# A cached-attention kernel on one core: two chunks of projection weights as two loads, two more chunks projected for all rows up front, and a warm-up that reads a constant

## The chip, the core and the metric

One NeuronCore of a Trainium2 chip. Time is device microseconds of one execution. The profile's "span" runs from the first to the last instruction of the core; most executions of these kernels take 1.7 to 1.9 us more than their span, and this difference ("time minus span") matters below. The engines are named as in the profile: PE (matrix engine; PEld are its weight loads), DVE, ACT, POOL, and SP, which issues nearly all DMA.

## The reference, cut to what matters

```python
# x (8, 32, 1024), k_cache and v_cache (8, 4, 8192, 128), wq (1024, 4096), wo (4096, 1024), all bf16
W = 2048                                                # the last 2048 positions of the cache
q = (x @ wq).reshape(B, Sq, 32, 128).transpose(0, 2, 1, 3)
k = repeat(k_cache[:, :, Sk - W:, :], 8); v = repeat(v_cache[:, :, Sk - W:, :], 8)
p = softmax(einsum("bhqd,bhkd->bhqk", q, k) * 128 ** -0.5)
out = einsum("bhqk,bhkd->bhqd", p, v).transpose(0, 2, 1, 3).reshape(8, 32, 4096) @ wo
```

## The kernel before

It works on 32 units (batch, key head). A unit is 16 key blocks: scores (`s_ps`), exponential on ACT, product with V (`o_ps`). Between them stand pieces of other work, such as the transposes of the next unit's keys (`tp`). "K2" is the key tile of unit 2, "V2" its value tile. Units 0 to 4 get their keys transposed by PE from `k_raw`.

The start matters here. The first group's weights come in eight chunks of 128 rows. Chunks 0 to 3 are projected for all 256 rows of x, chunks 4 to 7 only for the 128 rows that hold what the first unit needs (`Q_CUT = 4`); the rest is made up between the first score blocks (`q_rest`).

```python
Q_CUT = 4
N_WARM = (7, 0, 0)
V_HALVES = 29            # units from this one on load V as two halves
W_AT = (3, 3, 4, 4, ...) # after which unit's loads a later weight load is issued
...
    def load_v(self, ui, eng):
        ...
        n = self.KT // (2 if ui >= V_HALVES else 1)
        for j in range(0, self.KT, n):
            eng.dma_start(...)
...
    def start(self):
        warm = self.ps_s.tile([P, 512], FP32, name="warm_ps", tag="s_ps")
        wz = self.c1.tile([P, 512], BF16, name="wz")
        nc.vector.memset(wz[:, :], 0.0)
        ...
        nc.sync.dma_start(out=x_sb[:, 0, :], in_=xf[0:P, :])
        nc.scalar.dma_start(out=x_sb[:, 1, :], in_=xf[P:2 * P, :])
        wq0 = self.load_wq(0, 0, (1, 1, 2)) + self.load_wq(0, 1, (2, 1, 1))   # chunks per load
        for p in wq0[:4]:
            p()
        self.load_k(0, 0)          # first half of K0
        wq0[4]()
        wq0[5]()
        self.load_k(0, 1)
        self.load_v(0, nc.sync)
        self.load_k(1)
        self.load_v(1, nc.sync)
        ...
        def warm_up(n):
            for i in range(n):
                nc.tensor.matmul(warm[:, :], lhsT=wz[:, 0:P], rhs=wz[:, :], start=True, stop=True)
        warm_up(N_WARM[0])
        ... # x_turn: sixteen transposes of x, copied to xT
        for c in range(self.DC):                      # 8 chunks
            for h in range(self.rep):                 # 8 heads
                q_mm(c, h, 0, P if c >= Q_CUT else self.NQ)
            ...
            if c == self.DC - 3:
                ...
                k_turn(0)                             # transposes of K0, first half
                k_copy(0)
        k_turn(1)
        ...
        def q_rest(k):
            for h in (2 * k, 2 * k + 1):
                for c in range(Q_CUT, self.DC):
                    q_mm(c, h, P, self.NQ)
            q_copy("v", k, 1, self.B)
```

Of the kernel before, what the change touches and what calls it, by code (L numbers as in the profile page):

```python
# [11 lines left out]
BF16 = mybir.dt.bfloat16  # L12
# [3 lines left out]

RL_LIMIT = 1.0e22
RL_MIN = 1.0e-10
Q_CUT = 4
N_WARM = (7, 0, 0)  # L20
VA_ROW = 160
V_HALVES = 29

PE_T = (0, 1, 2, 3, 4)

# [79 lines left out]
class Fast:  # L105
# [93 lines left out]
    def load_v(self, ui, eng):  # L199
        b, g = self.units[ui]  # L200
        self.v_sb[ui] = self.vp.tile([self.P, self.KT, self.Dh], BF16, name="v_sb", tag="v")
        n = self.KT // (2 if ui >= V_HALVES else 1)
        for j in range(0, self.KT, n):
# [108 lines left out]
    def start(self):  # L312
        nc, P = self.nc, self.P
        warm = self.ps_s.tile([P, 512], FP32, name="warm_ps", tag="s_ps")
        wz = self.c1.tile([P, 512], BF16, name="wz")
        nc.vector.memset(wz[:, :], 0.0)
        x_sb = self.vp.tile([P, self.NT, self.D], BF16, name="x_sb", tag="v")
        xf = self.x.rearrange("b s d -> (b s) d")
        H = self.DC // 2

        nc.sync.dma_start(out=x_sb[:, 0, :], in_=xf[0:P, :])  # L321
        nc.scalar.dma_start(out=x_sb[:, 1, :], in_=xf[P:2 * P, :])
        wq0 = self.load_wq(0, 0, (1, 1, 2)) + self.load_wq(0, 1, (2, 1, 1))
        for p in wq0[:4]:
            p()
        self.load_k(0, 0)
        wq0[4]()
        wq0[5]()
        self.load_k(0, 1)
        self.load_v(0, nc.sync)  # L330
        self.load_k(1)
        self.load_v(1, nc.sync)
        self.weights = []
        for g in range(self.Hkv):
            if g + 1 < self.Hkv:
                self.weights += self.load_wq(g + 1, 0) + self.load_wq(g + 1, 1)
            if g:
                self.weights += self.load_wo(2 * g - 2) + self.load_wo(2 * g - 1)
        self.weights += self.load_wo(2 * self.Hkv - 2) + self.load_wo(2 * self.Hkv - 1)
        for ui in range(2, 4):  # L340
            self.load_unit(ui)
        for v in self.va:
            nc.gpsimd.memset(v[:, :, self.Dh:self.VW], 1.0)
        nc.gpsimd.memset(self.ones_c[:, :], 1.0)
        def warm_up(n):
            for i in range(n):
                nc.tensor.matmul(warm[:, :], lhsT=wz[:, 0:P], rhs=wz[:, :], start=True, stop=True)
        warm_up(N_WARM[0])


        def x_turn(half, pl, tag):
            ps = pl.tile([P, H, self.NT, P], BF16, name="xT_ps", tag=tag)
            for c in range(H):
                for t in range(self.NT):
                    c0 = (half * H + c) * P
                    nc.tensor.transpose(ps[:, c, t, :], x_sb[:, t, c0:c0 + P], self.ident[:, :])
            for i, copy in ((0, nc.vector.tensor_copy), (1, nc.scalar.copy)):
                c0 = half * H + i * H // 2
                copy(out=self.xT[:, c0:c0 + H // 2, :], in_=ps[:, i * H // 2:(i + 1) * H // 2, :, :].rearrange("p c t s -> p c (t s)"))

        x_turn(0, self.ps_m, "m")
        x_turn(1, self.ps_s, "s_ps")
        qs = [pl.tile([P, 2, self.NQ], FP32, name="q0_ps", tag=tag)
              for pl, tag in ((self.ps_o, "o_ps"), (self.ps_o, "o_ps"), (self.ps_m, "m"), (self.ps_m, "m"))]
        KT = self.KT
        tp = None

        def k_turn(half):
            for j in range(half * KT // 2, (half + 1) * KT // 2):
                nc.tensor.transpose(tp[:, j, :], self.k_raw[0][:, j, :], self.ident[:, :])  # L370

        def k_copy(half):
            sl = slice(half * KT // 2, (half + 1) * KT // 2)
            nc.vector.tensor_copy(out=self.kT[0][:, sl, :], in_=tp[:, sl, :])  # L374

        def q_mm(c, h, n0, n1):
            nc.tensor.matmul(qs[h // 2][:, h % 2, n0:n1], lhsT=self.wq_t[0, c // H][:, c % H, h * P:(h + 1) * P],  # L377
                             rhs=self.xT[:, c, n0:n1], start=(c == 0 and h % 2 == 0), stop=(c == self.DC - 1),
                             skip_group_check=True)

        for c in range(self.DC):
            for h in range(self.rep):
                q_mm(c, h, 0, P if c >= Q_CUT else self.NQ)
            if c == 0:
                warm_up(N_WARM[2])
                warm_sb = self.c1.tile([P, 8], BF16, name="warm_sb")
                nc.vector.tensor_copy(out=warm_sb[:, :], in_=warm[:, 0:8])
            if c == self.DC - 3:
                tp = self.ps_s.tile([P, KT, P], BF16, name="kf_ps", tag="s_ps")
                k_turn(0)  # L390
                k_copy(0)
        k_turn(1)

        def q_copy(eng, k, b0, b1):
            src = qs[k][:, :, :].rearrange("p h (b s) -> p b h s", b=self.B)[:, b0:b1, :, :]
            dst = self.q_view(0)[:, b0:b1, k * 2:(k + 1) * 2, :]
            (nc.vector.tensor_copy if eng == "v" else nc.scalar.copy)(out=dst, in_=src)  # L397
        for k, eng in ((0, "a"), (1, "v"), (2, "a"), (3, "v")):
            q_copy(eng, k, 0, 1)
        k_copy(1)  # L400
        self.va_copy(0)
# [6 lines that stand above are left out]
        self.q_rest = [lambda k=k: q_rest(k) for k in (0, 2, 3, 1)]  # L408
# [249 lines left out]
```

## Time and profile before

| | before |
|---|---|
| time, median of 6 executions | 186.74 us (186.40 to 186.98) |
| span of the profiled execution | 184.6 us |
| PE busy | 179.9 us, 97% |
| first scores | 13.38 us |

Lines of the page of before (the span; each engine with its busy us, share of the span and instructions; the engines of the chain that ended last):

```profile
span 184.6 us, 5089 instructions
...
PE 179.9 (97%) x2072; PEld 153.7 (83%) x2072; DVE 115.2 (62%) x267; ACT 131.8 (71%) x133; POOL 94.7 (51%) x150
...
PE 93%; DMA 4%; SPq 1%; DVE 1%; issue 0%
```

The last line is the chain of work that ended last: it is PE for 93% of the span, so a microsecond of PE saved anywhere without a new wait is a microsecond of the kernel. The 4% of DMA are the load of weights at the start that the chain runs through (2.12 to 8.65 us); PE itself stood still for the last 0.87 us of it. PE's timeline of before shows it (start, duration, operation, count, and in brackets how long the engine stood still before and for what):

```profile
1.20 3.17 PE L347 MATMUL warm_ps<-wz 128*128 128x512 bf16 x7 [1.20 <-DVE wz L316]
4.31 1.74 PE L356 MATMUL xT_ps<-ident,x_sb 128*128 128x128 bf16 x16
6.08 1.92 PE L377 MATMUL q_ps<-xT,wq_sb 128*128 128x256 bf16 x16
8.70 2.81 PE L377 MATMUL q_ps<-xT,wq_sb 128*128 128x256 bf16 x32 [0.70 <-DMA wq_sb<-in_wq_dram]
11.35 0.61 PE L370 MATMUL kf_ps<-ident,k_raw 128*128 128x128 bf16 x8
11.79 1.08 PE L377 MATMUL q_ps<-xT,wq_sb 128*128 128x128 bf16 x16
12.92 0.62 PE L370 MATMUL kf_ps<-ident,k_raw 128*128 128x128 bf16 x8
13.38 0.60 PE L469 MATMUL s_ps<-QT_63,kT 128*128 128x256 bf16 x4
13.82 1.06 PE L377 MATMUL q_ps<-xT,wq_sb 128*128 128x128 bf16 x16
...
16.04 0.60 PE L469 MATMUL s_ps<-QT_63,kT 128*128 128x256 bf16 x4
```

Read it by starts. The record of a matmul of 256 columns lasts 273 ns in the mean while the next one starts 109 ns after it, so ends overlap the next start, and the gap of 0.70 us before 8.70 is 0.87 us counted from where the next matmul could have started. The table by stage adds that DMA is full in this phase (stretch, busy us and count of each engine, clock, mean share of the DMA engines, GB/s):

```profile
4.00:10.00 6.00, 5.27 (x45) 4.16 (x45) 0.92 (x3) 1.17 (x2) 0.00 (x0) 1.00 0.99 293
...
14.00:19.00 5.00, 5.00 (x79) 4.83 (x77) 3.78 (x8) 4.06 (x4) 0.00 (x0) 1.00 1.03 406
...
29.00:184.60 155.60, 152.82 (x1745) 130.61 (x1742) 99.52 (x234) 115.98 (x116) 93.12 (x139) 1.00 1.01 268
```

### The profile page before, as it was taken

Reading aid. Unit: us, or ns where it says so; the run is one execution under the profiler, and the core shown is the slowest. Engines: PE = TensorE matmul, PEld = TensorE weight load, DVE = VectorE, ACT = ScalarE, POOL = GpSimd, SP = SyncE. Lnnn points to the kernel's source line nnn. Section 1 sums busy time; section 2 is a strip of 40 time slices with the busy share of each in tenths; the row PEclk is TensorE's granted clock in tenths of the full one; section 3 lists DMA queues with packets and bytes.
Section 4 is the critical chain, followed back from the end, with each engine's and each line's share of the span. In section 5 each row is a group of like instructions: output and inputs, shape, how many; then the busy total and the mean of one; then the engine's idle time right before and its main releaser. Section 6 shows DMA issues by size and latency. Waiting matters only on the chain.

```text
span 184.6 us, 5089 instructions
## 1 busy us (share of the span) xinstructions
PE 179.9 (97%) x2072; PEld 153.7 (83%) x2072; DVE 115.2 (62%) x267; ACT 131.8 (71%) x133; POOL 94.7 (51%) x150
## 2 busy tenths in 40 slices
PE   7899999999999999999999999999999999999994
PEld 2799999999999999987788899988787888888843
DVE  0238799994586686586467648656755865265363
ACT  2207899787789777777878677887877888888800
POOL 2000007949939959928954990797199379700000
PEclk9999999999999999999999999999999999999999
DMA  6999999999999989999999999999999999891003
GB/s 159 297 396 408 402 398 396 238 206 228 384 361 255 369 274 314 403 267 221 354 341 246 358 391 235 281 278 384 258 314 399 233 264 321 188 240 28 4 30 91
DMA packets 53082, 51.73 MB, mean 280 GB/s; under 512 B 39744, under 2 KB 40256, under 8 KB 53056
## 3 DMA queue, kind: packets, MB, share of 16 engines
q1 hardware_dynamic: 52480, 50.90, 98.9%
q10 hardware_dynamic: 576, 0.49, 0.8%
q8 instruction: 16, 0.26, 0.6%
q14 instruction: 10, 0.08, 0.2%
HBM read 41.42 MB, written 0.52 MB: 227 GB/s over the span
## 4 chain that ended last, share of the span: by engine, by line
PE 93%; DMA 4%; SPq 1%; DVE 1%; issue 0%
PE o_ps L480 31%; PE s_ps L469 30%; PE op_ps L295 15%; PE q_ps L275 11%; DMA wq_sb<-in_wq_dram 4%; PE q_ps L377 2%; PE tp L236 2%; PE kf_ps L370 1%; SPq L164 0%; DVE kT L374 0%; SPq L321 0%; DVE o_t L305 0%; DVE QT_63 L397 0%; PE cnt_ps L534 0%
## 5 line engine op out<-in xcount | busy, mean ns | idle before, releaser
L471 ACT ACTIVATE pT<-s_ps 128x1024 bf16<-128x1024 f32 x128 | 128.9, 1025 | 33.3 <-PE s_ps L469 32.3
L261 POOL TENSOR_SCALAR kTv<-kb 32x512 bf16<-32x512 bf16 x140 | 93.7, 670 | 65.1 <-PE s_ps L469 38.6
L480 PEld LDWEIGHTS <-pT 128*128 128x128 bf16 x1024 | 68.4, 98 | 3.2
L469 PEld LDWEIGHTS <-kT 128*128 128x128 bf16 x368 | 34.7, 98 | 10.4
L295 PE MATMUL op_ps<-wo_sb,OT 128*128 128x512 bf16 (+2 forms) x144 | 36.2, 356 | 0.0
L275 PE MATMUL q_ps<-xT,wq_sb 128*128 128x256 bf16 x192 | 28.1, 273 | 0.0
L480 PE MATMUL o_ps<-va_112,pT 128*128 128x129 bf16 x352 | 27.2, 220 | 0.0
L480 PE MATMUL o_ps<-va_113,pT 128*128 128x129 bf16 x352 | 27.0, 220 | 0.0
L480 PE MATMUL o_ps<-va_114,pT 128*128 128x129 bf16 x320 | 24.7, 220 | 0.0
L251 DVE STREAM_TRANSPOSE kb<-k_raw 128x512 bf16<-128x512 bf16 x36 | 23.8, 684 | 0.0
L417 DVE RECIPROCAL RL_all<-o_ps 128x2 f32<-128x2 f32 x32 | 5.3, 164 | 27.5 <-PE o_ps L480 27.5
L422 DVE TENSOR_SCALAR o_sb<-o_ps,RL_all 128x128 bf16<-128x128 f32 x64 | 19.5, 346 | 1.1
L469 PEld LDWEIGHTS <-kTv 128*128 128x128 bf16 x144 | 13.9, 98 | 5.1
L275 PEld LDWEIGHTS <-wq_sb 128*128 128x128 bf16 x192 | 17.0, 98 | 1.2
L469 PE MATMUL s_ps<-QT_63,kT 128*128 128x256 bf16 x112 | 16.8, 273 | 0.0
L424 DVE STREAM_TRANSPOSE OT<-o_sb 128x256 bf16<-128x256 bf16 x32 | 14.2, 445 | 1.1
L469 PE MATMUL s_ps<-QT_66,kT 128*128 128x256 bf16 x96 | 14.4, 273 | 0.0
L295 PEld LDWEIGHTS <-OT 128*128 128x128 bf16 x144 | 11.4, 98 | 2.3 <-DVE OT L424 0.2
L469 PE MATMUL s_ps<-QT_65,kT 128*128 128x256 bf16 x80 | 12.0, 273 | 0.0
L469 PE MATMUL s_ps<-QT_64,kT 128*128 128x256 bf16 x80 | 12.0, 272 | 0.0
L302 DVE TENSOR_TENSOR oacc<-op_ps,oacc 128x512 f32<-128x512 f32 x8 | 5.5, 682 | 7.4 <-PE op_ps L295 7.4
L411 DVE COPY va_113<-v_sb 128x2048 bf16<-128x2048 bf16 x11 | 9.5, 860 | 0.0
(45 smaller groups left out, 105.1 us busy)
## 6 DMA issues: line engine op xcount, KB each, us to landing
v_sb<-in_v_cache_dram SPq DMA_DIRECT2D x29, 512.0 KB, 6.9
wo_sb<-in_wo_dram SPq DMA_DIRECT2D x16, 512.0 KB, 6.8
wq_sb<-in_wq_dram SPq DMA_DIRECT2D x14, 512.0 KB, 6.9
k_raw<-in_k_cache_dram SPq DMA_DIRECT2D x13, 512.0 KB, 6.3
v_sb<-in_v_cache_dram SPq DMA_DIRECT2D x6, 256.0 KB, 6.5
wq_sb<-in_wq_dram SPq DMA_DIRECT2D x4, 256.0 KB, 6.4
kT<-in_k_cache_dram SPq DMA_TRANSPOSE x36, 6.8
k_raw<-in_k_cache_dram SPq DMA_DIRECT2D x2, 256.0 KB, 7.9
```

Of the source, the lines that this page charges most:

```text
L251: nc.vector.transpose(out=st["kb"][:, sl, :], in_=self.k_raw[ui][:, sl, :])
L261: nc.gpsimd.tensor_scalar(out=out, in0=in_, scalar1=1.0, scalar2=1.0, op0=ALU.mult, op1=ALU.mult)
L275: nc.tensor.matmul(st["ps"][:, 0:self.NQ], lhsT=self.wq_t[g, i][:, c % (DC // 2), hl * P:(hl + 1) * P], rhs=self.xT[:, c, :], start=(c == ...
L295: nc.tensor.matmul(ps[:, 0:w], lhsT=self.OT[:, gq, c, t * P:(t + 1) * P], rhs=self.wo_t[gq][:, c, n0:n0 + w], start=(k == 0), stop=(k == 7))
L302: nc.vector.tensor_tensor(out=acc, in0=ps[:, 0:w], in1=acc, op=ALU.add)
L411: self.nc.vector.tensor_copy(out=self.va[ui % 3][:, :, 0:self.Dh], in_=self.v_sb[ui][:, :, :])
L417: nc.vector.reciprocal(out=rl[:, ui * QT_N:(ui + 1) * QT_N], in_=o_ps[:, :, Dh])
L422: nc.vector.tensor_scalar(out=o_sb[:, qt, :, :], in0=o_ps[:, qt, 0:Dh].rearrange("p (i c) -> p c i", c=4), scalar1=rl[:, ui * QT_N + qt:ui ...
L424: nc.vector.transpose(out=self.OT[:, g * QT_N:(g + 1) * QT_N, :, b * self.Sq:(b + 1) * self.Sq], in_=o_sb[:, :, :, :])
L469: nc.tensor.matmul(s_ps[:, jj, :], lhsT=self.kT[ui][:, c * CJ + jj, :], rhs=q_u, start=True, stop=True)
L471: nc.scalar.activation(out=pT[:, :, :], in_=s_ps[:, :, :], func=ACT.Exp, bias=0.0, scale=self.scale)
L480: nc.tensor.matmul(o_ps[:, qt, 0:self.VW], lhsT=pT[:, jj, qt * P:(qt + 1) * P], rhs=va[:, j, 0:self.VW], start=(j == 0 and qt == 0), stop= ...
```

## The change

The intent: let PE go on with chunk 2 as soon as chunk 2 alone is there; fill the time in which PE would then wait for keys with projection work that has to be done anyway; start the warm-up without waiting for DVE's memset. V of unit 29 also becomes one load.

```diff
-Q_CUT = 4
-N_WARM = (7, 0, 0)
+Q_CUT = 6
+N_WARM = (8, 0, 0)
-V_HALVES = 29
+V_HALVES = 30
-        wz = self.c1.tile([P, 512], BF16, name="wz")
-        nc.vector.memset(wz[:, :], 0.0)
+        one = nc.const_aps.tensor
-        wq0 = self.load_wq(0, 0, (1, 1, 2)) + self.load_wq(0, 1, (2, 1, 1))
-        for p in wq0[:4]:
+        wq0 = self.load_wq(0, 0, (1, 1, 1, 1)) + self.load_wq(0, 1, (2, 1, 1))
+        for p in wq0[:5]:
             p()
         self.load_k(0, 0)
-        wq0[4]()
         wq0[5]()
+        wq0[6]()
-                nc.tensor.matmul(warm[:, :], lhsT=wz[:, 0:P], rhs=wz[:, :], start=True, stop=True)
+                nc.tensor.matmul(warm[:, :], lhsT=one(1.0, [P, P], BF16), rhs=one(1.0, [P, 512], BF16), start=True, stop=True)
```

## The prediction

> **What bounds the kernel now.** The matrix engine: the page gives PE 97% of the 184.6 us span, and the chain that ended last is 93% PE; its only long wait is a DMA of projection weights (4%) at the start. In the first 30 us DMA is the second limit: the table by stage shows a DMA share of about 1.0 from 3 us on (400 GB/s after 10 us).
>
> **The start now (timeline, single records of the trace).** Warm-up matmuls start at 1.20 us, 426 ns apart; x lands at 4.44. The transposes of x go 107 ns apart and 55 ns only from 5.7 us: half clock until then (Trainium skill, "TensorE: Matmul & The Clock Gate", Part 1, the HAM clock gate; this trace agrees). Weights land: chunk 0 at 6.03, 1 at 6.72, 2+3 at 8.65, 4+5 at 10.0; the second half of K0 at 12.88. PE issues chunk 1 until 7.83 and stands until 8.70 (0.87 us), later 0.21 us more for K0. First scores at 13.38.
>
> **What the change does.**
> 1. Chunk 2 alone should land at about 7.75 (half-way from 6.72 to 8.65; an estimate). PE goes on at 7.83, ends chunk 3 at about 9.57, then waits for chunks 4+5 until about 10.1: 0.87 us of gap goes, about 0.5 comes back.
> 2. Chunks 4 and 5 for all rows: 16 matmuls of 109 ns instead of 56, +0.85 us before the first scores; 16 of 56 ns fewer after them, -0.89. Neutral in work; but otherwise step 1's time would end in the wait for K0. First scores at about 13.7, yet about -0.55 us at 18 us.
> 3. Warm-up without the memset starts at about 0.9; eight end at about 4.3 as seven did. The first projection still waits for chunk 0: nothing, unless the clock rises earlier.
> 4. V of unit 29 as one load: 0.
>
> **How much survives.** DMA carries the same bytes and is full, so later landings stay. K2 lands at 19.29 and is used at 19.60 (slack 0.3); K4 lands at 28.40 and is used at 28.51 (slack 0.1). One of the 16 parts of these loads is 1.28 us late; instruction fetches of 1.1 us at 16.83 and 24.16 stand just before. So of 0.55 us most should turn into new waits for K2 and K4 in a run like the profiled one (186.33 us), leaving 0.1. Executions that are slower at the start (186.94, 186.98) have more slack and keep more.
>
> **Prediction.** 186.35 us, range 185.8 to 186.8. Chances: faster by over 2% 0.01, within 2% 0.98, slower 0.01.
>
> **What would show it.** Right: warm-up from 0.9 us; chunk 2's projection at 7.8 to 7.9; a wait of 0.3 to 0.7 us before chunk 4, none for K0; rest matmuls in groups of 8, not 16; new PE waits for k_raw of units 2 and 4 at about 19 and 28 us, ending at today's landings. Wrong: no such waits (then the gain should be 0.5 us or more), or a wait for chunk 2.
>
> **What would make it wrong.** An instruction fetch that falls on another load or engine would free K2 or K4 (gain up to 0.6 us) or delay them 1.28 us more. The split could make the loads of the first 10 us, at only 240 to 400 GB/s, faster or slower as a whole. An earlier full clock could help by tenths; DVE, dense at 14 to 18 us, could become a new wait.

## The result, and the profile after

The changed kernel took 186.38 us (median of 6, 186.02 to 187.18) against 186.74 us (median of 6). The ratio is 0.9985, with a 95% interval of 0.9962 to 1.0008: within noise. Ratios are computed as the mean time of one kernel's runs over the mean of the other's in the same rounds, so they are not quite the ratios of the medians quoted. The prediction was 186.35.

PE's timeline of after:

```profile
0.78 3.57 PE L346 MATMUL warm_ps<-const-bfloat16-1.0 128*128 128x512 bf16 x8 [0.78 <-PEq L641]
4.37 2.00 PE L355 MATMUL xT_ps<-ident,x_sb 128*128 128x128 bf16 x16
6.26 2.10 PE L376 MATMUL q_ps<-xT,wq_sb 128*128 128x256 bf16 x16
8.62 3.92 PE L376 MATMUL q_ps<-xT,wq_sb 128*128 128x256 bf16 x32 [0.25 <-DMA wq_sb<-in_wq_dram]
12.37 0.61 PE L369 MATMUL kf_ps<-ident,k_raw 128*128 128x128 bf16 x8
12.82 1.06 PE L376 MATMUL q_ps<-xT,wq_sb 128*128 128x128 bf16 x16
13.79 0.62 PE L369 MATMUL kf_ps<-ident,k_raw 128*128 128x128 bf16 x8
14.25 0.60 PE L468 MATMUL s_ps<-QT_63,kT 128*128 128x256 bf16 x4
14.69 0.61 PE L376 MATMUL q_ps<-xT,wq_sb 128*128 128x128 bf16 x8
...
16.07 0.60 PE L468 MATMUL s_ps<-QT_63,kT 128*128 128x256 bf16 x4
```

The pieces moved as intended: the warm-up starts at 0.78 instead of 1.20, and the rest group has 8 matmuls instead of 16. But first scores come at 14.25, not at the forecast 13.7. Two things came later in this execution: the clock (single records: the transposes and the first two projections ran at half rate, until 6.6 us; in before until 5.7), and the weights (chunk 2 landed at 8.57, chunks 4+5 at 10.57 instead of 10.00), and with them the second half of K0 (13.75 instead of 12.88). At the third block of scores after stands at 16.07 and before at 16.04, and the two profiles then run in step to the end: the same span (lines of the page of after):

```profile
span 184.6 us, 5057 instructions
...
PE 180.7 (98%) x2057; PEld 154.0 (83%) x2057; DVE 115.1 (62%) x266; ACT 131.7 (71%) x133; POOL 95.0 (51%) x150
```

So one pair of profiles says "nothing gained at the start, no waits for K2 or K4 either", which is not the story that was predicted, although the time was right: "no such waits" stood in the prediction as a sign that it is wrong. The experiments had to tell whether this was one unlucky execution.

### The profile page after: what moved, and what is told of

It is laid out like the page before. It is cut to its first block, busy times and chain, and to the rows that moved or that the text cites. A ratio compares the mean times of both kernels' runs of the same rounds, so it can differ in the third digit from the quotient of the medians.

```text
span 184.6 us, 5057 instructions
## 1 busy us (share of the span) xinstructions
PE 180.7 (98%) x2057; PEld 154.0 (83%) x2057; DVE 115.1 (62%) x266; ACT 131.7 (71%) x133; POOL 95.0 (51%) x150
## 4 chain that ended last, share of the span: by engine, by line
PE 93%; DMA 4%; SPq 1%; issue 0%; DVE 0%
PE o_ps L479 31%; PE s_ps L468 30%; PE op_ps L295 15%; PE q_ps L275 11%; DMA wq_sb<-in_wq_dram 4%; PE q_ps L376 2%; PE tp L236 2%; SPq L164 1%; PE kf_ps L369 1%; SPq L320 0%; DVE o_t L305 0%; PE cnt_ps L533 0%
## 5 line engine op out<-in xcount | busy, mean ns | idle before, releaser
L468 PE MATMUL s_ps<-QT_63,kT 128*128 128x256 bf16 x112 | 16.8, 272 | 0.0
L468 PE MATMUL s_ps<-QT_66,kT 128*128 128x256 bf16 x96 | 14.4, 273 | 0.0
```

The source lines that it names most:

```text
L468: nc.tensor.matmul(s_ps[:, jj, :], lhsT=self.kT[ui][:, c * CJ + jj, :], rhs=q_u, start=True, stop=True)
```

## The experiments

They ran as three groups of four, each on another chip, so a kernel is compared with before of its own group (11 executions; 6 of each kernel). Spans are means of those executions. "Third scores" is the start of the third block of scores in the profiled execution (16.04 in before), and "PE end" is the start of the last matmul against 181.60 in the first profile of before. Landings, clock and single starts are read from the trace's single records.

| kernel | ratio, 95% interval | span, and before's | third scores, shift | PE end, shift | PE end to span end |
|---|---|---|---|---|---|
| before (profile) | | | 16.04 | 181.60 | 2.95 |
| after (profile) | 0.9985 (0.9962 to 1.0008) | 184.57 | +0.03 | +0.04 | 2.93 |
| e1_split | 1.0031 (1.0017 to 1.0046) | 185.15, 184.51 | +0.39 | +0.39 | 3.40 |
| e2_qcut | 1.0010 (0.9991 to 1.0030) | 184.47, 184.51 | -0.58 | -0.58 | 2.97 |
| e3_warm | 1.0000 (0.9983 to 1.0016) | 184.53, 184.51 | +0.19 | +0.19 | 2.95 |
| e4_split_qcut | 1.0038 (1.0017 to 1.0059) | 185.00, 184.51 | -0.59 | -0.10 | 3.41 |
| a_v29 | 1.0021 (1.0001 to 1.0041) | 184.83, 184.66 | -0.27 | +0.03 | 3.42 |
| e1b_split_v30 | 1.0012 (0.9991 to 1.0032) | 184.80, 184.66 | -0.04 | -0.04 | 2.94 |
| k_before | 1.0008 (0.9988 to 1.0027) | 184.73, 184.66 | -0.05 | -0.05 | 2.95 |
| k_after | 0.9976 (0.9959 to 0.9993) | 184.23, 184.66 | +0.12 | +0.13 | 2.93 |
| a2_after | 1.0005 (0.9984 to 1.0026) | 184.40, 184.82 | -0.79 | -0.37 | 3.04 |
| e5_no_warm | 0.9990 (0.9964 to 1.0016) | 184.25, 184.82 | -0.32 | -0.30 | 2.93 |
| a_pad | 0.9969 (0.9951 to 0.9987) | 184.32, 184.82 | -0.29 | +0.11 | 2.93 |
| k_after_pad | 0.9982 (0.9963 to 1.0001) | 184.45, 184.82 | -0.55 | -0.34 | 2.92 |

A profile shows one execution, and executions of one kernel spread over 0.4 to 1.3 us of span; so shifts explain where time goes within an execution, and only the means say what a kernel gains.

### First group: the parts of the change

Three theories stand in the expectations. A: the start gains, and waits for keys that land no earlier take the gain back. B: the split makes the early loads later as a whole. C: only the moment at which PE's clock rises differs between executions.

**e1_split**: the loads alone.

```diff
-        wq0 = self.load_wq(0, 0, (1, 1, 2)) + self.load_wq(0, 1, (2, 1, 1))
+        wq0 = self.load_wq(0, 0, (1, 1, 1, 1)) + self.load_wq(0, 1, (2, 1, 1))
 # cut: the calls that issue these loads, renumbered as in the change
```

> Chunks 2 and 3 as two loads, nothing else. Theory A (late K landings limit): chunk 2's projection starts within 0.2 us of chunk 1's end (in before a gap of 0.87 us), but the time so won ends in the waits for chunks 4+5 (about 10.1) and for the second half of K0 (12.9); first scores stay at 13.3 to 13.5, time within 0.1 us of before. Theory B (the split makes the early loads later as a whole, as the profile of after suggests with chunks 4+5 landing at 10.57 instead of 10.0): chunks 4+5 land at 10.3 or later and first scores come 0.2 us or more later, time 0.1 to 0.4 us above before. Theory C (only the moment at which the clock rises differs between runs): chunks 4+5 land where they do in before, and differences follow the clock.

Measured: 0.31% slower, the clearest result of the group and expected by no theory in this size. In its profile, chunk 2 starts at 7.86 with no gap (as A said), but chunks 4+5 landed at 10.27 and first scores come at 13.77, 0.39 us late (nearer to B); and the mean span is 0.64 us longer. The rest is in the last column of the table: after the last matmul, 3.40 us pass to the end instead of 2.95. What SP waits for in the last 5 us shows the difference (the view of waits: us in total, times, longest). First before:

```profile
SPq L653 <- DMA out_dram<-o_t: 1.1, 3, 0.4
```

The same view of e1_split:

```profile
SPq L653 <- DMA out_dram<-o_t: 1.6, 1, 1.6
```

In before SP waits three times, in between the landings of the last output transfers; in e1_split once, until all have landed. The single records tell the order. At the end SP looks at eight DMA semaphores in a fixed order, and each look takes about 0.063 us:

```
before:    SP looks at 182.11 182.18 182.25 182.31 182.64 183.03 183.20 183.68; last output landed 183.66; drain 183.74
e1_split:  SP looks at 184.08 184.15 184.21 184.28 184.34 184.40 184.46 184.52; last output landed 184.06; drain 184.59
```

In before the transfer that lands last has the semaphore looked at last. One load more in the program shifts the assignment by one, the last transfer falls on the semaphore that is looked at first, and the seven other looks come after it: 7 x 0.063 = 0.44 us. This "tail theory" makes V of unit 29 important: going from two loads to one, it takes away exactly the one load that the split adds.

**e2_qcut**: chunks 4 and 5 for all rows, loads as in before.

```diff
-Q_CUT = 4
+Q_CUT = 6
```

> Chunks 4 and 5 for all rows, loads as in before. Theory A: the gap before chunk 2 stays near 0.9 us, first scores at about 13.98 (+0.6), but 0.89 us less after them: PE is about 0.3 us ahead at 18 us, and K2 (19.3) or K4 (28.4) takes most of it: 0 to 0.3 us below before. Theory B: the same or better than the whole change, 0.3 us below before, since the loads are not split. Theory C: nothing but the clock.

Measured: no difference (1.0010), in the span neither. Its profiled execution was a good one: the gap before chunk 2 was only 0.25 us, PE stood 0.58 us ahead at the third scores, and kept it, since here K2 landed at 18.71 and K4 at 27.80, both before they were needed. Most executions of these kernels take 1.7 to 1.9 us more than their span ("time minus span"). But this execution, with the shortest span seen (184.0 us), took 186.68 us: 2.68 us more than its span. Another of its six did the same. That is a second effect that nobody expected; a_pad below is about it.

**e3_warm**: the warm-up alone.

> Warm-up of eight from the constant tile, nothing else. Theory A: starts at 0.8 instead of 1.2 us, x's transposes start within 0.1 us of before, first projection waits for chunk 0: time within 0.1 us of before. Theory C: the clock rises at a moment that varies by up to some us between runs whatever the warm-up is, so here too anywhere from 4.5 to 8 us; if an earlier warm-up makes it rise earlier on average, 0.1 to 0.3 us below before.

```diff
-N_WARM = (7, 0, 0)
+N_WARM = (8, 0, 0)
-        wz = self.c1.tile([P, 512], BF16, name="wz")
-        nc.vector.memset(wz[:, :], 0.0)
+        one = nc.const_aps.tensor
     # and the matmul's operands as in the change
```

Measured: 1.0000. The warm-up starts at 0.78, the transposes at 4.26, and the first matmuls at full rate come at 6.01 (5.72 in before). No effect that these runs resolve, as predicted.

**e4_split_qcut**: both, with the old warm-up and V of unit 29 in two loads.

> Split and chunks 4 and 5 together, old warm-up. Theory A: as the whole change, 0.2 to 0.5 us below before in the mean; first scores 0.3 later than before, PE 0.3 to 0.55 us ahead at 18 us where the clock rose at the same moment as in before, then waits for K2 or K4. Theory B: no faster than chunks 4 and 5 alone, chunks 4+5 land at 10.3 or later. Theory C: gains of 0.3 or more only where the clock rises early.

Measured: 0.38% slower. 0.45 us is tail (3.41 us), and two of six executions took 2.7 to 2.8 us more than their span. Without the tail its mean span is 184.55, as before's 184.51, so the 0.2 to 0.5 us that theory A expected in the mean are missing. Its profile is the clean case of theory A's waits. PE is 0.59 us ahead at the third scores, and then two waits appear that before does not have (PEld's timeline of e4_split_qcut around 19 and 28 us):

```profile
19.30 0.23 PEld L236 LDWEIGHTS <-k_raw 128*128 128x128 bf16 x4 [0.31 <-DMA k_raw<-in_k_cache_dram]
...
28.39 0.23 PEld L236 LDWEIGHTS <-k_raw 128*128 128x128 bf16 x4 [0.18 <-DMA k_raw<-in_k_cache_dram]
```

The same transposes in before (PE's timeline) have no wait in front of them:

```profile
19.60 0.39 PE L236 MATMUL tp<-ident,k_raw 128*128 128x128 bf16 x4
...
28.51 0.39 PE L236 MATMUL tp<-ident,k_raw 128*128 128x128 bf16 x4
```

K2 landed at 19.26 and K4 at 28.35, nearly where they did in before (19.29 and 28.40). PE's lead goes from 0.59 to 0.28 to 0.10 us. Those are the two waits and the remainder of 0.1 us that the prediction named.

### Second group: the tail, and the keys

**a_v29**: the whole change with V of unit 29 in two loads again.

```diff
-V_HALVES = 30
+V_HALVES = 29
```

> The whole change, but V of unit 29 as two loads again: one load more in the program. Tail theory (the last output transfer then falls on the first of the semaphores that the sync engine waits for at the end, and the seven other waits come after it, 0.065 us each, as in the two runs with the split alone): from the last matmul's start to the end of the span 3.4 us instead of 2.92, about 0.45 us slower than the whole change. Rival (V of unit 29 is off the chain, worth nothing): same as the whole change, tail 2.92 us.

Measured: tail 3.42 us; 0.21% slower than before. The whole change itself was not run in this group. What SP waits for in the last 5 us is again a single wait, as in e1_split:

```profile
SPq L652 <- DMA out_dram<-o_t: 1.6, 1, 1.6
```

The tail theory holds. (PE also waited for K2 and K4 in this profile, 0.12 and 0.18 us, and its lead of 0.27 us ended at nothing.)

**e1b_split_v30**: the split alone, with V of unit 29 in one load.

```diff
 # e1_split, and
-V_HALVES = 29
+V_HALVES = 30
```

> Chunks 2 and 3 as two loads, V of unit 29 as one. Tail theory: tail back at 2.92 to 2.96 us and time within 0.15 us of before, so the 0.6 us that the split alone lost were 0.45 of tail and the rest chance of the loads. Rival (the split slows the start by itself): still 0.3 to 0.6 us slower, first scores at 13.7 or later.

Measured: tail back at 2.94 us, with three waits of SP again:

```profile
SPq L653 <- DMA out_dram<-o_t: 1.0, 3, 0.4
```

The time is 1.0012, not distinguishable from before: the split alone shows no gain, and without the tail no cost that these runs resolve. Its profile shows why it gains nothing alone: no gap before chunk 2, first scores at 13.34 all the same (13.38 in before), because the second half of K0 landed at 12.84.

```profile
6.19 4.98 PE L377 MATMUL q_ps<-xT,wq_sb 128*128 128x256 bf16 x48
11.01 0.61 PE L370 MATMUL kf_ps<-ident,k_raw 128*128 128x128 bf16 x8
11.46 1.36 PE L377 MATMUL q_ps<-xT,wq_sb 128*128 128x128 bf16 x16
12.89 0.62 PE L370 MATMUL kf_ps<-ident,k_raw 128*128 128x128 bf16 x8
13.34 0.49 PE L469 MATMUL s_ps<-QT,kT 128*128 128x256 bf16 x3
```

Forty-eight projections run without a break; the time won stands before 12.89. Theory B (a split slows the loads) stays open. Over the ten profiles with the split, chunks 4+5 landed between 9.3 and 10.7 us, over the four without between 9.9 and 10.0, with means of 10.1 and 9.95. But the second half of K0 landed at a mean of 13.25 us in the ten (12.84 to 13.75) and 12.86 in the four (12.66 to 13.06), and in PE's order its transposes stand before the first scores. The same count of loads that made the tail is at work here. SP's loads take eight semaphores in turn, and one that comes round to a semaphore in use is issued only after the landing that it belongs to. For the second half of K0 that is the landing of x without the split (issued at 4.84 to 5.00 us) and the landing of chunk 0 with it (issued at 5.40 to 6.56 us). In e1_split SP waited 0.3 us for weights before it, which it did not in before. That the later issue makes the later landing is not shown; no run took the one without the other.

**k_before, k_after**: K2 loaded ahead of V1, and the next weights after K4 and V4. Both kernels got the same edit.

```diff
-W_AT = (3, 3, 4, 4, ...
+W_AT = (4, 4, 4, 4, ...
         self.load_k(1)
+        self.load_k(2)
         self.load_v(1, nc.sync)
 # and unit 4's weight loads ahead of unit 8's keys; load_unit(2) without its load_k
```

> Before, with K2 loaded ahead of V1, and the next group's four weight loads after K4 and V4 instead of two of them ahead: K2 should land about 1.3 us earlier and K4 about 2.6 us earlier. Nothing waits for K2 or K4 in before, so theory A expects the time of before, within 0.1 us. If instead executions of before also lose time there now and then, it becomes faster by 0.1 to 0.2.

> The whole change with the same earlier K2 and K4. Theory A (the gain at the start is taken back by waits for K2 and K4): no such waits any more, and what PE is ahead at 18 us stays to the end: 0.3 to 0.6 us below before. Rival (the gain is lost in the first 14 us already, by weights that land later and a clock that rises later): the same as the whole change, 0 to 0.3 below before.

Measured: k_before 1.0008, no difference, although K2 landed at 16.66 us and K4 at 25.66 (19.29 and 28.40 in before). k_after 0.9976 (0.9959 to 0.9993): faster, mean span 0.43 us below before's. No wait for any `k_raw` stands in its profile, but that execution had a late start (third scores +0.12), so it had none to avoid. On its own, k_after looked like support for theory A; the third group took that back.

### Third group: the late instruction fetch, and the total

The group's question: why do some executions take up to 2.9 us more than their span? The DMA view of e2_qcut after its span's end (184.0 us) has one transfer in it, on the queue of instructions (queue, kind: packets, MB, share):

```profile
DMA packets 1, 0.02 MB, mean 3 GB/s; under 512 B 0, under 2 KB 0, under 8 KB 0
...
q8 instruction: 1, 0.02, 1.4%
```

It is one packet of 16 KB, from 185.79 to 186.92 us by the records. Every profile has 16 such packets. In before, e1_split, e3_warm, e1b_split_v30 and k_before the last one comes at 174.0 to 174.5 us. In the kernels with `Q_CUT = 6`, which have 30 to 32 matrix-engine instructions fewer (one pair of a load and a matmul for each projection that is no longer cut in two), it comes at 180.1 to 180.5 or at 185.8 to 186.7, after the end. Which engine's instructions the packet holds is not told. The four profiled executions in which it came after the end (e2_qcut, e4_split_qcut, k_after, e5_no_warm) took 2.5 to 2.8 us more than their span; all the others 1.77 to 1.84. The Trainium skill, "Runtime: NRT & Kernel Launch", section "Instruction fetch mechanics", says that an engine fetches its instructions in blocks of 16 KiB, 256 instructions, over a DMA queue of its own; the 16 KB packets agree.

**a2_after** and **e5_no_warm**: the whole change again, and the change with the old warm-up.

> The whole change once more, a second sample and trace. Theory A: mean span within 0.15 us of before's or up to 0.3 below; if this profile's early start is good (first scores before 13.8 us), waits for K2 or K4 appear in it; if it is not, the first scores are late and there are none.

> The whole change without the new warm-up (seven from the cleared tile, as before). If the warm-up is worth nothing: same mean as the whole change within 0.15 us. If it raises the clock earlier on average: 0.1 to 0.3 us slower than the whole change, and its clock rises later in the profile. The tail is 2.92 to 2.96 us.

Measured: a2_after 1.0005 in time, although its mean span is 0.42 us below before's (at most 0.3 was expected): three of its six executions took 2.3 to 2.8 us more than their span. In its profile the start was good: no wait before chunk 2 or 4, PE 0.79 us ahead at the third scores; then it waited 0.35 us for K4 (landed 28.09) and kept 0.37:

```profile
28.13 0.23 PEld L236 LDWEIGHTS <-k_raw 128*128 128x128 bf16 x4 [0.35 <-DMA k_raw<-in_k_cache_dram]
```

e5_no_warm: span 0.57 below, time 0.9990, three of six executions with 2.5 to 2.9. Old and new warm-up cannot be told apart: by the trace's clock records, or the spacing of matmuls where it has none, the clock rose between 4.4 and 7.1 us in the seven profiles with the old one and between 3.5 and 6.7 in the seven with the new one.

**a_pad**: the whole change, the warm-up cut into more and shorter matmuls, so that the instruction count is before's.

```diff
-N_WARM = (8, 0, 0)
+N_WARM = (23, 0, 0)
-                nc.tensor.matmul(warm[:, :], lhsT=one(1.0, [P, P], BF16), rhs=one(1.0, [P, 512], BF16), start=True, stop=True)
+                nc.tensor.matmul(warm[:, 0:178], lhsT=one(1.0, [P, P], BF16), rhs=one(1.0, [P, 178], BF16), start=True, stop=True)
```

> The whole change with its warm-up cut into 23 matmuls of 178 columns instead of 8 of 512: as much warm-up, and as many matrix-engine instructions as before has (4224 instead of 4194). Theory: with 30 fewer the last instruction fetch comes at 180 us or later instead of 174, and in some executions after the last instruction, where it adds 0.5 to 1 us outside of the span. Then with the pad the last fetch is at about 174 us again and no execution has more than 1.95 us between time and span (of 30 executions of kernels with 30 to 32 fewer that I have seen, eight had over 1.95 us; of those with before's number none); mean time 0.1 to 0.2 us below the whole change. Rival (chance): still one or two in six over 1.95 us.

Measured: 0.9969 (0.9951 to 0.9987), mean time 186.10 us against 186.60 of a2_after and 186.61 of before in the same rounds: 0.50 us below the whole change, more than the 0.1 to 0.2 expected. All six executions took 1.75 to 1.82 us more than their span, and the last fetch came at 174.34 us. The DMA view of a_pad from 173 to 176 us has it:

```profile
q8 instruction: 1, 0.02, 1.9%
```

Counted over all timed runs of the three groups and the first comparison: of 42 executions of kernels with fewer instructions, 14 took over 1.95 us more than their span; of 69 with before's number or the pad, none (at most 1.88); the first comparison's executions of before have no span on record and are not among them. Its mean span, 184.32, is that of the whole change within noise, so the pad acts outside of the span, as the theory says.

**k_after_pad**: the pad, and K2 and K4 earlier.

> The whole change with K2 and K4 loaded earlier, and the pad. Theory A with both: no waits for K2 or K4, no late fetch, mean time 0.4 to 0.6 us below before, and faster than the whole change and than the pad alone by 0.1 to 0.3 us. Rival (loss in the first 14 us): as the pad alone.

Measured: 0.9982 (0.9963 to 1.0001), mean 186.22 us: 0.40 us below before, at the edge of what was expected, and not faster than the pad alone. Theory A's second half fails here. In both padded profiles K2 and K4 are not waited for, but K1 is (PEld's timeline of a_pad):

```profile
17.02 0.45 PEld L236 LDWEIGHTS <-k_raw 128*128 128x128 bf16 x8 [0.39 <-DMA k_raw<-in_k_cache_dram]
```

K1 landed at 16.98 (15.44 in before). An instruction fetch came at 14.83 us instead of 16.83, and one of K1's sixteen parts landed 1.0 us after the others. In k_after_pad the fetch came at 14.39, K1 landed at 16.53 and was waited for 0.21 us. That the pad makes the fetch early is not shown: it came at 14.76 in a2_after and 14.99 in e3_warm, without the pad, and there V1 was late and K1 was not. So which load is late differs between executions, and moving K2 and K4 forward does not help an execution in which it is K1.

## Why the prediction was right or wrong, point by point

- **The time (186.35; measured 186.38)** was right, and so was "within 2%" and the reason in its large outline: PE bounds, the start is worth half a microsecond, and it survives only in part. Part of the agreement is luck. In the spans more survived (0.42 us in the mean of the third group) than the 0.1 us forecast for a run like the profiled one, and the late instruction fetch, which was left out, took 0.24 us of it back; and the tail of 0.45 us, which the split alone would have cost, was not seen, but V of unit 29 happens to take it away. The measured gain itself is within noise, so it cannot confirm the forecast one.
- **Step 1, split loads**: right in most profiles. Chunk 2 without a gap in six of the eight profiles that have the split and not the pad (and in both padded ones); the wait before chunk 4 is 0 to 0.5 us, and in some a gap of 0.1 to 0.4 us stands before chunk 3 instead. In the profile of after itself it was not so (0.42 us gap by starts, chunk 2 landed at 8.57 instead of 7.75): the landings of the first 10 us vary by more than a microsecond between executions. "None for K0" does not hold always: PE stood 0.17 us for K0 in e4_split_qcut and 0.25 in a2_after.
- **Step 2, neutral in work, and needed for step 1**: right. The split alone gives first scores at 13.34 instead of 13.38; with both they came at 13.4 to 14.3 us in eight profiles (forecast 13.7). Full-row projections go 109 ns apart and halves 56 ns; "TensorE: Matmul & The Clock Gate" of the Trainium skill (section "Back-to-back issue gap") gives N/2.4 + 2.5 ns, which is 109 and 56 for 256 and 128 columns: the trace agrees. The section calls this the gap of an isolated matmul and gives about 81 ns at 128 columns for a stream with weight loads; here each of these matmuls has its weight load (96 and 96 records of L377 in before), and 56 ns is what was measured.
- **Step 3, warm-up**: right, no effect that can be resolved (1.0000 alone, interval 0.9983 to 1.0016).
- **Step 4, "V of unit 29 as one load: 0"**: wrong in its size. What it does alone was not run, but together with the split it is worth 0.45 us: it keeps the number of loads, and with it the order in which the last semaphores are looked at. The step that failed is that I asked what the load feeds, not what its number shifts.
- **"Most of it should turn into new waits for K2 and K4"**: seen as predicted in e4_split_qcut (0.59 us ahead, 0.31 and 0.18 waited, 0.10 left), for K4 in a2_after and a_v29, not in after, e2_qcut or e5_no_warm. But the mean span of the changed kernel in the third group is 0.42 us below before's, and moving K2 and K4 earlier gave no further gain that could be measured. So the waits are real and the statement "most" was too strong. How much they take in the mean stays open; differences under about 0.3 us are not resolved by these runs.
- **A term that was missing**: the late instruction fetch. 2.03 us is the mean of time minus span over the 12 executions of the whole change, against 1.79 for the 33 of before in the groups. So 0.24 us of what the span gains is lost again in the mean. "An instruction fetch that falls on another load" stood among the risks, and did happen (K1 in the padded kernels); that fewer instructions would move the last fetch past the end was not seen.
- **Open**: why the last fetch came at 180 us in three of the seven unpadded profiles with `Q_CUT = 6` and at 186 in four (the whole change, profiled twice, had 180 both times); whether the split delays the second half of K0; and whether the split helps at all in the mean beside `Q_CUT`, since e4_split_qcut without its tail was level with before on one chip and e5_no_warm 0.57 us below on another.

## What to carry to other kernels

A start that waits for loads pays only as far as the next loads are early, so follow PE's lead through the next two or three tiles and ask of each what its landing leaves. Compare spans and times separately: a change can shorten the span and lose it after the last instruction, and here restoring the instruction count with a finer warm-up (0.9969, faster than both kernels) kept the gain. Where a program rotates a few DMA semaphores, adding a single load changes which of them the end waits for, and at the start which landing the issue of a later load waits for; count the loads, and check the last 3 us of the profile after any change to them.

## What the Trainium skill lacked or had wrong

- "Runtime: NRT & Kernel Launch", "Instruction fetch mechanics", calls the cost of crossing a 16 KiB boundary mostly hidden. Here a fetch of 16 KB is one packet of about 1.0 us (median of 224); in before one sixteenth of K2 landed 1.30 us after the other parts (19.29 against 17.99) behind the fetch at 16.83 us. In 13 of 14 profiles one part of load after load was 0.6 to 1.3 us late from the first fetch (14.4 to 16.8 us) on, until 25 to 27 us, and in the profile of after none was. In the four profiles with a fetch after the last instruction, time minus span was 2.5 to 2.8 us against 1.77 to 1.84 in the others.
- No page has what the end of the kernel's own program costs: SP's looks at the eight DMA semaphores cost about 0.063 us each, so whether the last transfer's semaphore is looked at first or last is worth about 0.45 us (tail 3.40 to 3.42 us against 2.92 to 3.04 us, profiles of 3 kernels against 11).
- "TensorE: Matmul & The Clock Gate", Part 1, says that the moment at which the clock rises varies by 500 ns either way between runs. In these fourteen profiles it rose between 3.5 and 7.1 us, 2.7 to 5.9 us after the start of the warm-up, and in two profiles of the same kernel (after and a2_after) at 6.67 and 3.78 us; its own note on the varying number of cold matmuls fits better.
